# Sorted-block attention feeding a maxout MoE: the MoE of one batch interleaved with the attention of the next, v sorted from a rearranged copy, xT read strided from PSUM, q transposed in column tiles

## The chip, the cores and the metric

The kernel runs on one core of one Trainium2 chip. The time is the device time of one launch in microseconds (us). The engines of the core are TensorE (PE for its matmuls, PEld for its weight loads), VectorE (DVE), ScalarE (ACT), GpSimd (POOL) and SyncE (SP). A weight load puts the stationary operand into the array, and the matmul behind it streams the moving operand past it.

## The reference

With 4 batches, 8 heads, 768 positions and 64 dimensions per head, the positions are cut into 8 blocks of 96. A Sinkhorn iteration makes an 8 by 8 matrix P per head, P mixes the blocks of k and of v, each q block attends to the mixed k and v block of its own index, and the result feeds a two-way maxout layer. P is `sort_net` at the start.

```python
for _ in range(5):
    P = np.exp(P - P.max(-1, keepdims=True))
    P = P / (P.sum(-1, keepdims=True) + 1e-09)
    P = P / (P.sum(-2, keepdims=True) + 1e-09)
k_sorted = np.einsum('bhij,bhjcd->bhicd', P, k_b)     # v_sorted likewise
scores = scale * np.matmul(q_b, k_sb.transpose(0, 1, 2, 4, 3))
attn = softmax(scores)
x = np.matmul(attn, v_sb)                             # to (3072 tokens, 512)
g = np.maximum(x @ w1, x @ w2)                        # 512 -> 1024
out = g @ w_out                                       # 1024 -> 512
```

## The kernel before

The work is done per batch of 768 tokens; k and v are loaded and sorted for two batches at a time (`sb` 0 is batches 0 and 1, `sb` 1 is batches 2 and 3). max(h1, h2) is computed as h2 + relu(x(w1 - w2)), and h2 @ w_out is folded into one matrix wc = w2 @ w_out, so that the MoE has one hidden product (`moe_h`) and an output product with two parts (`moe_out`).

The order of all instructions is the order in which the Python code issues them (the schedule is manual). Each engine runs its own queue strictly in that order. All PSUM tiles share one pool of 4 buffers of two banks, used in rotation, so the fifth tile waits until the first has been copied out. The copies out of PSUM that go through `evac` (L81) are given to ACT or DVE by a running sum of estimated costs (`load`, `pick`, L72 to L79).

The parts are:

- The five Sinkhorn iterations (L167) and the building of the block-diagonal matrices `bd_v` and `bd_k` from P (L189 to L224), for both `sb` together, before anything else on PE.
- `q_transposes(b, half)` (L232): `pair_q` (L98) first lets DVE bring the two heads of a pair side by side, then 12 transposes of 128x128 per half put q into `qT`.
- `sort_k(sb, t)` (L254), 6 steps of 32 small matmuls in two diagonal quarters of the array, and `sort_v(sb, t)` (L275), 8 steps of 8 matmuls. The weights of a `sort_v` matmul are 96 columns of `v_raw`, 64 elements (128 bytes) apart: `vv[:, :, t * 8 + n]`.
- `scores(b, u)` (L294), 8 matmuls with weights of 64 rows and 96 columns, then one exponential on ACT. `values(b, u)` (L318), 8 matmuls with weights of 96 columns, then a reciprocal and a multiplication on DVE, which leave the tile `x`. A 65th column of ones in `v_sb` gives the softmax sum. There are 8 of each per batch.
- `x_transposes(b, hp)` (L347), 4 per batch: 8 transposes of `x` and one ACT copy into `xT` that brings the positions into order on the way. It reads PSUM in sequence and writes 2-byte elements 12 bytes apart.
- `w2_transposes`, `w_product` and `w_difference` (L371 to L411) make wc and w1 - w2 once.
- `moe_h(b, ch, t)` (L416), 8 per batch, and `moe_out(b, ti)` (L441), 6 per batch: 14 units per batch.

The top level (L490 to L554) does the attention of batches 0 and 1 with the weight work in between, then issues the 56 MoE units and hands out the list `rest` (sort of `sb` 1, attention of batches 2 and 3) between units 6 to 27, that is, within the MoE of batches 0 and 1. The MoE of batches 2 and 3 follow alone. In `attention_steps` (L478) `values` comes two steps behind its `scores`, and `x_transposes` directly behind the second of its two `values`.

All input loads are issued on POOL's queue in the order q of batch 0, k, v, q of batch 1, w2, w_out, w1; the loads for batches 2 and 3 follow as soon as their buffers are read out. The output is stored from SP's queue.

Of the kernel before, what the change touches and what calls it, by code (L numbers as in the profile page):

```python
# [15 lines left out]
def kernel(  # L16
# [80 lines left out]

    def pair_q(b):  # L98

        t = qpool.tile([128, HP, R, 2, D], BF16, tag="q_pair", name="q_pair")  # L100
        for par in range(2):
            nc.vector.tensor_copy(
                out=t[:, :, :, par, :],
                in_=q_raw[b].rearrange("p (a t) (r d) -> p a r t d", t=2, d=D)[:, :, :, par, :],
            )
# [76 lines left out]


    maskJ = const.tile([128, NB], FP32, tag="maskJ", name="maskJ")
    nc.vector.reduce_sum(
        out=maskJ, in_=ident.rearrange("p (m j) -> p j m", j=NB), axis=AX.X
    )
    bd_v, bd_k = [], []
    for sb in range(NSB):  # L189
        sel = const.tile([G, 2, 8, NB], BF16, tag=f"sel{sb}", name=f"sel{sb}")  # L190
        src = ident[0:G, sb * 16 : sb * 16 + 16].rearrange("p (gp par) -> p par gp", par=2)
        for par in range(2):
            nc.vector.tensor_copy(
                out=sel[:, par], in_=src[:, par, :].to_broadcast([G, 8, NB])
            )
# [151 lines left out]
    def x_transposes(b, hp):  # L347
        ps = ps_bf16("tx_ps")
        for ih in range(2):
# [235 lines left out]
```

## Time and profile before

| | us |
|---|---|
| median of three runs | 245.03 (244.81 to 247.16) |
| the profiled execution, whole | 243.13 |
| its span, from the first to the last instruction | 241.1 |
| PE busy in the span | 194.1 |
| ACT busy, DVE busy | 110.3, 88.2 |

[...] The whole time is 2.03 us longer than the span. The durations below come from that one execution.

### The profile page before, as it was taken

The page shows a single profiled execution, that of the slowest core. Times are in us where ns is not written, and L with a number is a line of the kernel's source. Part 1 is how long each engine was busy: PE and PEld are TensorE (multiplying, and loading weights), DVE is VectorE, ACT ScalarE, POOL GpSimd, SP SyncE. Part 2 cuts the span into 40 slices and gives each one's busy share as a digit, 9 for nine tenths or more (in the row PEclk, how much of TensorE's full clock was granted, in tenths as well). Part 3 has the DMA queues.
Part 4 walks back from the last instruction along what each step waited for, and adds up shares of the span by engine and source line. Part 5 has one row for each costly group of instructions (what it writes and reads, how often), then busy time and mean ns, then how long its engine had stood idle before and what let it go on. Part 6 is the DMA issues. An engine that isn't in the chain of part 4 may idle for free.

```text
span 241.1 us, 4147 instructions
## 1 busy us (share of the span) xinstructions
PE 194.1 (81%) x1846; PEld 128.2 (53%) x1858; DVE 88.2 (37%) x159; ACT 110.3 (46%) x98; POOL 18.1 (8%) x35
## 2 busy tenths in 40 slices
PE   0037697867869579999999677898979999999983
PEld 0036696756744435777765455654444654465431
DVE  4755275442620660523322545454133312023210
ACT  3108413977584275643152656946575320142010
POOL 8450312110000000000000000000000000000000
PEclk9999655575758959999999979999999999999999
DMA  5999999999800000000110200000120202220132
GB/s 70 211 222 200 210 205 209 211 223 203 138 3 0 0 0 3 3 4 13 74 58 32 87 3 0 0 3 23 67 87 6 84 0 87 87 90 0 48 126 87
DMA packets 11952, 19.13 MB, mean 79 GB/s; under 512 B 1696, under 2 KB 6816, under 8 KB 11680
## 3 DMA queue, kind: packets, MB, share of 16 engines
q0 software_dynamic: 8608, 12.59, 29.0%
q1 hardware_dynamic: 3328, 6.30, 6.8%
q8 instruction: 14, 0.23, 0.4%
q14 instruction: 2, 0.02, 0.0%
HBM read 25.17 MB, written 6.29 MB: 131 GB/s over the span
## 4 chain that ended last, share of the span: by engine, by line
PE 67%; DVE 15%; ACT 12%; issue 4%; DMA 1%; DVEq 0%; ACTq 0%
PE out_ps L458 17%; PE h_ps L422 16%; PE v_ps L279 9%; PE out_ps L450 8%; ACT xT L361 7%; DVE x L338 5%; PE o_ps L325 3%; PE wc_ps L395 3%; PE s_ps L301 3%; PE tx_ps L353 2%; PE tq_ps L239 2%; PE k_ps L262 2%; ACT kT L83 2%; PE tw_ps L375 1%; DVE o L85 1%
## 5 line engine op out<-in xcount | busy, mean ns | idle before, releaser
L361 ACT COPY xT<-tx_ps 128x768 bf16<-128x768 bf16 x16 | 43.5, 2722 | 25.2 <-PE tx_ps L353 25.2
L422 PE MATMUL h_ps<-xT,w_sb 128*128 128x384 bf16 x256 | 47.1, 341 | 1.0 <-DVE w_sb L405 0.9
L458 PE MATMUL out_ps<-wo_sb,g 128*128 128x512 bf16 x192 | 45.4, 379 | 0.1
L422 PEld LDWEIGHTS <-w_sb 128*128 128x128 bf16 x256 | 25.2, 101 | 19.1 <-issue 2.5
L309 ACT ACTIVATE e<-s_ps 96x768 bf16<-96x768 f32 x32 | 26.0, 845 | 12.2 <-PE s_ps L301 12.2
L458 PEld LDWEIGHTS <-g 128*128 128x128 bf16 x192 | 18.8, 98 | 22.7
L432 ACT ACTIVATE g<-h_ps 128x768 bf16<-128x768 f32 x21 | 17.4, 830 | 24.9 <-PE h_ps L422 24.9
L450 PE MATMUL out_ps<-wc,xT 128*128 128x512 bf16 x85 | 23.3, 379 | 1.4 <-DVE o L85 0.8
L353 PE MATMUL tx_ps<-ident,x 96*128 96x96 bf16 x128 | 12.2, 232 | 13.7 <-DVE x L338 12.8
L85 DVE COPY o<-out_ps 128x1024 f32<-128x1024 f32 (+1 forms) x8 | 9.3, 1158 | 36.2 <-PE out_ps L458 36.2
L338 DVE TENSOR_TENSOR x<-o_ps,rs 96x512 bf16<-96x512 f32 x32 | 22.0, 687 | 1.1
L325 PE MATMUL o_ps<-v_sb,e 96*96 96x65 bf16 x256 | 18.9, 225 | 4.1 <-ACT xT L361 2.5
L279 PEld LDWEIGHTS <-v_raw 128*96 128x96 bf16 x128 | 21.6, 257 | 0.5
L279 PE MATMUL v_ps<-bv,v_raw 128*96 128x128 bf16 x128 | 21.7, 347 | 0.0
L325 PEld LDWEIGHTS <-e 96*96 96x96 bf16 x256 | 16.9, 141 | 6.6 <-issue 2.5
L85 DVE CAST v_sb<-v_ps 96x1024 bf16<-96x1024 f32 x10 | 12.2, 1221 | 21.9 <-PE v_ps L279 21.6
L301 PE MATMUL s_ps<-qT,kT 64*96 64x96 bf16 x256 | 13.5, 240 | 6.9 <-issue 1.9
L434 DVE TENSOR_SCALAR g<-h_ps 128x768 bf16<-128x768 f32 x11 | 10.5, 958 | 21.0 <-PE h_ps L422 21.0
L83 ACT COPY o<-out_ps 128x1024 f32<-128x1024 f32 (+1 forms) x5 | 4.6, 927 | 28.0 <-PE out_ps L458 28.0
L336 DVE RECIPROCAL rs<-o_ps 96x8 f32<-96x8 f32 x32 | 6.4, 200 | 29.2 <-PE o_ps L325 29.1
L353 PEld LDWEIGHTS <-x 96*128 96x128 bf16 x128 | 7.9, 110 | 17.0 <-DVE x L338 15.6
L301 PEld LDWEIGHTS <-kT 64*96 64x96 bf16 x256 | 10.0, 144 | 11.2 <-issue 8.0
(51 smaller groups left out, 128.6 us busy)
## 6 DMA issues: line engine op xcount, KB each, us to landing
out_dram<-o SPq DMA_DIRECT2D x11, 512.0 KB, 2.8
q_raw<-in_q_dram POOLq DMA_DIRECT2D x4, 768.0 KB, 16.8
k_raw<-in_k_dram POOLq DMA_DIRECT2D x12, 256.0 KB, 12.2
v_raw<-in_v_dram POOLq DMA_DIRECT2D x4, 768.0 KB, 16.0
w_sb<-in_moe_w_dram POOLq DMA_DIRECT2D x4, 512.0 KB, 19.4
wo_sb<-in_moe_w_out_dram POOLq DMA_DIRECT2D x2, 512.0 KB, 21.8
out_dram<-o SPq DMA_DIRECT2D x2, 256.0 KB, 2.0
p_sb<-in_sort_net_dram SPq DMA_DIRECT2D x1, 8.0 KB, 1.6
```

The lines of the kernel that those rows point to most:

```text
L85: nc.vector.tensor_copy(out=out_ap, in_=in_ap)
L279: nc.tensor.matmul(ps[0:BLK, n * 128 : (n + 1) * 128], vv[:, :, t * 8 + n], bd_v[sb], start=True, stop=True,)
L301: nc.tensor.matmul(ps[0:BLK, h2 * 512 + ii * BLK : h2 * 512 + (ii + 1) * BLK], kT[h2 * 64 : h2 * 64 + 64, gp * 8 + i, :], qT[b][h2 * 64 : ...
L309: nc.scalar.activation(out=e, in_=ps[0:BLK].rearrange("p (t f) -> p t f", t=2)[:, :, 0 : 4 * BLK], func=AF.Exp, scale=scale,)
L325: nc.tensor.matmul(ps[0:BLK, h2 * 512 + ii * 65 : h2 * 512 + (ii + 1) * 65], e[:, h2, ii * BLK : (ii + 1) * BLK], v_sb[:, h2 * 64 + gp * 8 ...
L338: nc.vector.tensor_tensor(out=x.rearrange("p i t d -> p t i d"), in0=ov[:, :, :, 0:D], in1=rs.to_broadcast([BLK, 2, 4, D]), op=ALU.mult,)
L353: nc.tensor.matmul(ps[:, i * BLK : (i + 1) * BLK], x[:, ii].rearrange("p t d -> p (t d)"), ident[0:BLK, 0:BLK], is_transpose=True, start=True,
L361: nc.scalar.copy(out=xT[:, hp, b * S : (b + 1) * S].rearrange("p (i c r) -> p i r c", r=R, c=PB), in_=ps[:, 0:S].rearrange("p (i r c) -> p ...
L422: nc.tensor.matmul(ps[:, m * 512 : m * 512 + TCH], w1_sb[:, hp, fb * 128 : (fb + 1) * 128], xT[:, hp, tok0 : tok0 + TCH], start=(hp == 0), ...
L432: nc.scalar.activation(out=g, in_=src, func=AF.Relu)
L450: nc.tensor.matmul(dst, xT[:, hp, tok0 : tok0 + 128], wc[:, hp, :], start=(hp == 0), stop=False,)
L458: nc.tensor.matmul(dst, g_tiles[b, ch, fb // 2][:, fb % 2, off : off + 128], wo_sb[:, fb, :], start=False, stop=(fb == NFB - 1),)
```

## The change

- Order: only batch 0 is attended before the MoE begins. The attention of batch b+1 (for batch 2 with the sort of `sb` 1 ahead of it) is handed out between the 14 MoE units of batch b; the MoE of batch 3 stands alone.
- In `attention_steps`, `values` comes three steps behind its `scores`, and `x_transposes` at least one `values` behind its second `x`.
- v is first copied by `turn_v` into `v_dc`, where the 96 positions of one dimension lie together: 4 copies on DVE for `sb` 0, and 4 copies on POOL for `sb` 1, issued behind the load of the last q.
- The weights of `sort_v`, `scores` and `values` are read 128 columns wide (32 of them beyond the block, their results unused), so 32 spare columns are set to zero at the ends of `kT`, `v_dc` and of eight fixed `e` buffers that replace the pool.
- `q_transposes` no longer pairs heads on DVE; each 128x128 transpose becomes two with 64 columns of weights, which write the two halves of the PSUM partitions.
- `x_transposes` copies out with a strided read of PSUM and a write in sequence, by ACT or DVE as `evac` chooses.
- Sinkhorn and selections are interleaved, `bd_v` and `bd_k` are built separately for each `sb`, and q of batch 0 is transposed ahead of them. The identity and the mask are made ahead of the load of k.

```diff
-    def pair_q(b):
...
+    kT = big.tile([128, 64 * BLK + 32], BF16, tag="kT", name="kT")
+    nc.vector.memset(kT[:, 64 * BLK :], 0.0)
+    v_dc = big.tile([128, D * BLK + 32], BF16, tag="v_dc", name="v_dc")
...
         for n in range(2 * R):
             hp, r = half * 2 + n // R, n % R
-            nc.tensor.matmul(
-                ps[:, n * 128 : (n + 1) * 128],
-                q_pair[b][:, hp, r].rearrange("p t d -> p (t d)"),
+            for h2 in range(2):
+                nc.tensor.matmul(
+                    ps[h2 * 64 : h2 * 64 + 64, n * 128 : (n + 1) * 128],
+                    qv[:, 2 * hp + h2, r, :],
...
+    def turn_v(eng, t, parts):
+        n = D // parts
+        eng.tensor_copy(
+            out=v_dc[:, t * n * BLK : (t + 1) * n * BLK].rearrange("p (d c) -> p d c", c=BLK),
+            in_=v_raw.rearrange("p (c d) -> p d c", d=D)[:, t * n : (t + 1) * n, :],
+        )
...
-                ps[0:BLK, n * 128 : (n + 1) * 128],
-                vv[:, :, t * 8 + n],
+                ps[:, n * 128 : (n + 1) * 128],
+                v_dc[:, (t * 8 + n) * BLK : (t * 8 + n) * BLK + 128],
                 bd_v[sb],
...
-                    kT[h2 * 64 : h2 * 64 + 64, gp * 8 + i, :],
+                    kT[h2 * 64 : h2 * 64 + 64, (gp * 8 + i) * BLK : (gp * 8 + i) * BLK + 128],
...
-                    e[:, h2, ii * BLK : (ii + 1) * BLK],
+                    e[:, (h2 * 4 + ii) * BLK : (h2 * 4 + ii) * BLK + 128],
...
-        nc.scalar.copy(
-            out=xT[:, hp, b * S : (b + 1) * S].rearrange("p (i c r) -> p i r c", r=R, c=PB),
-            in_=ps[:, 0:S].rearrange("p (i r c) -> p i r c", r=R, c=PB),
-        )
-        load["A"] += 800
+        evac(
+            xT[:, hp, b * S : (b + 1) * S].rearrange("p (i c r) -> p i c r", r=R, c=PB),
+            ps[:, 0:S].rearrange("p (i r c) -> p i c r", r=R, c=PB),
+            S,
+        )
...
-        for u in range(8 + 2):
+        for u in range(8 + 4):
             if u < 8:
                 steps.append(lambda u=u: scores(b, u))
-            if u >= 2:
-                steps.append(lambda u=u: values(b, u - 2))
-                if u % 2 == 1:
-                    steps.append(lambda u=u: x_transposes(b, (u - 2) // 2))
+            if 3 <= u < 8 + 3:
+                steps.append(lambda u=u: values(b, u - 3))
+            if u >= 5 and u % 2 == 1:
+                steps.append(lambda u=u: x_transposes(b, (u - 5) // 2))
...
+    for t in range(4):
+        turn_v(nc.vector, t, 4)
     for t in range(8):
         sort_v(0, t)
+        if t % 2 == 1:
+            scores(0, 4 + t // 2)
+    for u in range(8):
         values(0, u)
+        if u >= 2 and u % 2 == 0:
+            x_transposes(0, u // 2 - 1)
     for t in range(2):
         w2_transposes(t)
+    x_transposes(0, 3)
     for t in range(2):
         w_product(t)
     load_q(2)
     load_k(1, 3)
     load_v(1)
     load_q(3)
+    for t in range(4):
+        turn_v(nc.gpsimd, t, 4)
     for t in range(2):
         w_difference(t)
+    between = [
+        q_steps(1) + attention_steps(1),
+        q_steps(2) + sort_steps(1) + attention_steps(2),
+        q_steps(3) + attention_steps(3),
+        [],
+    ]
     for b in range(B):
...
+        steps, done = between[b], 0
+        for n, unit in enumerate(units):
+            unit()
+            want = -(-len(steps) * (n + 1) // (len(units) - 1))
+            while done < min(want, len(steps)):
+                steps[done]()
+                done += 1
```

DVE's queue around the first sort of v, ahead of the first `values`: kT, v_sb and v_dc are copies, rs and x belong to `values`. Before:

```order
L85 COPY qT<-tq_ps 128x1536
L85 CAST kT<-k_ps 128x64x16 x2
L85 CAST v_sb<-v_ps 96x128x8 x6
L336 RECIPROCAL rs<-o_ps 96x8
L338 TENSOR_TENSOR x<-o_ps,rs 96x2x4x64
```

And now:

```order
L85 CAST kT<-k_ps 128x64x16 x3
L202 TENSOR_TENSOR pm_452<-pe,maskJ 128x64
L209 TENSOR_REDUCE pt_454<-pm_452 128x8
L211 TENSOR_TENSOR bv_456<-mask_92,pt_454 128x128
L218 TENSOR_TENSOR bk_458<-bv_456 128x64
L285 COPY v_dc<-v_raw 128x1536 x4
L85 CAST v_sb<-v_ps 96x128x8 x6
L350 RECIPROCAL rs<-o_ps 96x8
L352 TENSOR_TENSOR x<-o_ps,rs 96x2x4x64
```

All four turning copies stand ahead of all six of DVE's casts of sorted v, in the same queue.

POOL's queue at its end: the loads, w_sb being w1 and w2. Before:

```order
L138 DMA w_sb<-in_moe_w_dram 128x2x1024 x2
L95 DMA q_raw<-in_q_dram 128x8x384
L118 DMA k_raw<-in_k_dram 64x1x2048 x6
L125 DMA v_raw<-in_v_dram 64x1x6144 x2
L95 DMA q_raw<-in_q_dram 128x8x384
```

And now:

```order
L127 DMA w_sb<-in_moe_w_dram 128x2x1024 x2
L95 DMA q_raw<-in_q_dram 128x8x384
L107 DMA k_raw<-in_k_dram 64x1x2048 x6
L114 DMA v_raw<-in_v_dram 64x1x6144 x2
L95 DMA q_raw<-in_q_dram 128x8x384
L285 COPY v_dc<-v_raw 128x1536 x4
```

The four copies of the second v stand behind the load of the last q, whose buffer is read by the q transposes of batch 1.

PE's queue where the transposes of an attention begin that runs beside the MoE, with buffer numbers. Before, in batch 2: the second x that tx_ps_1723 takes is made from o_ps_1710.

```order
L325 MATMUL o_ps_1710<-v_sb_182,e_1613 96x65
L325 LDWEIGHTS e_1613
L325 MATMUL o_ps_1710<-v_sb_182,e_1613 96x65
L353 LDWEIGHTS x_1686
L353 MATMUL tx_ps_1723<-ident_96,x_1686 128x96
```

And now, in batch 1: the second x that tx_ps_1087 takes, x_1040, is made from o_ps_1029.

```order
L436 MATMUL h_ps_1076<-xT_138,w1_sb_82 128x384
L436 LDWEIGHTS w1_sb_82
L436 MATMUL h_ps_1076<-xT_138,w1_sb_82 128x384
L367 LDWEIGHTS x_1006
L367 MATMUL tx_ps_1087<-ident_87,x_1006 128x96
```

Before, the transposes followed at once on the product that the second x comes from; now h_ps_1042, s_ps_1053, o_ps_1063 and h_ps_1076 stand between o_ps_1029 and them.

## Rows read from the trace of the kernel before

**Rows 1.** Busy time by engine in stretches: us, PE, PEld, DVE, ACT, POOL, clock, DMA.

```profile
39.00:59.00 20.00, 14.72 (x181) 12.86 (x182) 9.21 (x20) 15.33 (x12) 2.82 (x5) 0.59 1.14 215
...
71.00:87.00 16.00, 12.14 (x85) 6.19 (x84) 6.60 (x11) 7.92 (x4) 0.00 (x0) 0.82 0.00 0
...
124.00:184.40 60.40, 50.89 (x507) 31.32 (x511) 23.96 (x43) 38.34 (x30) 0.00 (x0) 0.97 0.09 36
184.40:237.40 53.00, 51.97 (x269) 26.47 (x271) 11.34 (x11) 10.44 (x14) 0.00 (x0) 1.00 0.17 65
237.40:241.10 3.70, 0.00 (x0) 0.00 (x0) 0.00 (x0) 0.58 (x1) 0.00 (x0) 0.97 0.18 71
```

**Rows 2.** Who waited for whom: us in total, times, longest.

```profile
PE tx_ps L353 <- DVE x L338: 12.8, 17, 1.6
```

**Rows 3.** Groups by line and shape: busy us, mean ns | idle before, releaser.

```profile
L361 ACT COPY xT<-tx_ps 128x768 bf16<-128x768 bf16 x16 | 43.5, 2722 | 25.2 <-PE tx_ps L353 25.2
L338 DVE TENSOR_TENSOR x<-o_ps,rs 96x512 bf16<-96x512 f32 x32 | 22.0, 687 | 1.1
L336 DVE RECIPROCAL rs<-o_ps 96x8 f32<-96x8 f32 x32 | 6.4, 200 | 29.2 <-PE o_ps L325 29.1
L434 DVE TENSOR_SCALAR g<-h_ps 128x768 bf16<-128x768 f32 x11 | 10.5, 958 | 21.0 <-PE h_ps L422 21.0
L85 DVE CAST v_sb<-v_ps 96x1024 bf16<-96x1024 f32 x10 | 12.2, 1221 | 21.9 <-PE v_ps L279 21.6
L83 ACT CAST v_sb<-v_ps 96x1024 bf16<-96x1024 f32 x6 | 6.1, 1021 | 16.7 <-PE v_ps L279 16.7
L102 DVE COPY q_pair<-q_raw 128x1536 bf16<-128x1536 bf16 x8 | 4.3, 573 | 0.2 <-issue 0.2
L279 PEld LDWEIGHTS <-v_raw 128*96 128x96 bf16 x128 | 21.6, 257 | 0.5
L325 PEld LDWEIGHTS <-e 96*96 96x96 bf16 x256 | 16.9, 141 | 6.6 <-issue 2.5 <-DVE v_sb L85 1.5 <-ACT e L309 0.2
L422 PEld LDWEIGHTS <-w_sb 128*128 128x128 bf16 x256 | 25.2, 101 | 19.1 <-issue 2.5 <-DVE w_sb L405 1.8
```

**Rows 4.** POOL in order of time: start, us, what [idle before, releaser].

```profile
5.63 0.29 POOL masks.py:197 MEMSET ident<- 128x128 bf16 x1
...
24.02 0.71 POOL L138 DMA_DIRECT2D w_sb<-in_moe_w_dram  x1 [6.58 <-DMA v_raw<-in_v_dram]
```

**Rows 5.** The chain that ended last, in order of time: start, us, what.

```profile
59.48 3.43 PE tw_ps L375 x32
...
71.97 7.48 PE wc_ps L395 x30
79.48 1.23 DVE wc L85
...
84.84 2.36 DVE w_sb L405 x2
...
96.58 1.34 PE tq_ps L239 x24
...
99.22 1.64 PE k_ps L262 x96
...
184.53 10.40 PE h_ps L422 x64
...
210.47 10.40 PE h_ps L422 x64
```

**Rows 6.** PE in order of time, 171.2 to 172.8 us: start, us, what.

```profile
171.21 0.38 PE L301 MATMUL s_ps<-qT,kT 64*96 64x96 bf16 x8
171.52 0.55 PE L325 MATMUL o_ps<-v_sb,e 96*96 96x65 bf16 x8
171.90 1.03 PE L450 MATMUL out_ps<-wc,xT 128*128 128x512 bf16 x4
```

**Rows 7.** Input loads by line: count, KB each, median us from issue to landing.

```profile
w_sb<-in_moe_w_dram POOLq DMA_DIRECT2D x4, 512.0 KB, 19.4
```

More of the change, by code (lines that the diff above doesn't have):

```diff
@@ L89 @@
     nc.sync.dma_start(out=p_sb, in_=sort_net.rearrange("b h i j -> (b h) i j"))
-    q_raw, q_pair, qT = {}, {}, {}
+    q_raw, qT = {}, {}
     def load_q(b):
@@ L96, in load_q @@
         q_raw[b] = t
-    def pair_q(b):
[L100 to L104, printed above, removed]
-            )
-        load["D"] += 1000
-        q_pair[b] = t
     k_raw = big.tile([128, BLK * D], BF16, tag="k_raw", name="k_raw")
@@ L166, with sinkhorn @@
     p_bf = const.tile([G, NB, NB], BF16, tag="p_bf", name="p_bf")
-    for it in range(5):
+    maskJ = const.tile([128, NB], FP32, tag="maskJ", name="maskJ")
+    sels = []
+    def sinkhorn(it):
         nc.scalar.activation(out=p_sb, in_=p_sb, func=AF.Exp)
@@ L181, with selections, block_diagonals @@
         )
[L184 to L195, printed above, removed]
+    def selections():
+        nc.vector.reduce_sum(
+            out=maskJ, in_=ident.rearrange("p (m j) -> p j m", j=NB), axis=AX.X
+        )
+        for sb in range(NSB):
+            sel = const.tile([G, 2, 8, NB], BF16, tag=f"sel{sb}", name=f"sel{sb}")
+            src = ident[0:G, sb * 16 : sb * 16 + 16].rearrange("p (gp par) -> p par gp", par=2)
+            for par in range(2):
+                nc.vector.tensor_copy(
+                    out=sel[:, par], in_=src[:, par, :].to_broadcast([G, 8, NB])
+                )
+            sels.append(sel)
+    bd_v, bd_k = {}, {}
+    def block_diagonals(sb):
         pe = ps_f32("pe")
@@ L307, in scores @@
                 )
-        e = epool.tile([BLK, 2, 4 * BLK], BF16, tag="e", name="e")
+        e = e_bufs[(b * 8 + u) % NE]
         nc.scalar.activation(
-            out=e,
+            out=e[:, 0 : 8 * BLK].rearrange("p (t f) -> p t f", t=2),
             in_=ps[0:BLK].rearrange("p (t f) -> p t f", t=2)[:, :, 0 : 4 * BLK],
@@ L526 @@
     load_q(3)
+    for t in range(4):
+        turn_v(nc.gpsimd, t, 4)
     for t in range(2):
         w_difference(t)
-    rest = []
-    for half in range(2):
-        rest.append(lambda half=half: q_transposes(2, half))
-    for t in range(6):
-        rest.append(lambda t=t: sort_k(1, t))
-    for t in range(8):
-        rest.append(lambda t=t: sort_v(1, t))
-    rest += attention_steps(2)
-    for half in range(2):
-        rest.append(lambda half=half: q_transposes(3, half))
-    rest += attention_steps(3)
-    units = []
-    for b in range(B):
-        units += [lambda b=b, t=t: moe_h(b, 0, t) for t in range(4)]
-        units += [lambda b=b, t=t: moe_h(b, 1, t) for t in range(4)]
-        units += [lambda b=b, ti=ti: moe_out(b, ti, b == B - 1 and ti >= 4) for ti in range(6)]
-    hold, span = 5, 2 * 14 - 1
-    done = 0
-    for n, unit in enumerate(units):
-        unit()
-        want = len(rest) * max(0, n + 1 - hold) // (span - hold)
-        while done < min(want, len(rest)):
-            rest[done]()
-            done += 1
+    between = [
[3 more added lines that the diff above has]
+        [],
+    ]
+    for b in range(B):
+        units = [lambda t=t: moe_h(b, 0, t) for t in range(4)]
+        units += [lambda t=t: moe_h(b, 1, t) for t in range(4)]
+        units += [lambda ti=ti: moe_out(b, ti, b == B - 1 and ti >= 4) for ti in range(6)]
+        steps, done = between[b], 0
[5 more added lines that the diff above has]
+                done += 1
 _INS = ['q', 'k', 'v', 'sort_net', 'moe_w1', 'moe_w2', 'moe_w_out']
```

68 lines of the change are left out of this document (32 added, 36 removed).

## The prediction

> **What bounds the kernel now.** I read the table of busy time by stretch first, then the waits, then the groups by line. In the last 53 us, the MoE of batches 2 and 3, PE is busy 51.97 us at the full clock [rows 1]: PE is the bound there and nothing beside it matters. [...] The waits name whom: x transposes waited for DVE's `x` 17 times, 12.8 us in all [rows 2], since they follow directly on the product that `x` is made from. The groups by line name the second: the ACT copy into xT takes 2722 ns for 768 elements, where the DVE pass over 768 elements of g takes 958 [rows 3]. So the MoE units are solid, and the time to be had lies in the attention and in all that comes before the first MoE unit, which starts behind the two `w_difference` passes, at 84.84 + 2.36 = 87.2 us [rows 5].
>
> **The change, along the time of the new order.** The new time is built up stage by stage, since nearly everything moves.
>
> *Until v is there.* POOL's load queue shows the first v load landed at 24.0 us, by the wait that ended then [rows 4]. The order of loads up to there is the same, and the identity and mask that go ahead of k cost POOL about 1 us while the load of q is still running, so I keep 24.0. Sinkhorn, q transposes, the sort of k and the first four scores move about among themselves before that, and I give them no gain: v is late next.
>
> *Turning v on DVE.* Four copies of 1536 elements, which no row shows with this read 128 bytes apart. From the g pass (768 elements, 958 ns) and the v_sb cast (1024, 1221 ns) an element costs 1.03 ns, so that 1536 take 958 + 768 x 1.03 = 1.75 us [rows 3]. Below, the q_pair copy of 1536 elements in runs of 64 took 0.57 us [rows 3]. Above, the weight load of v with the same spacing took 257 ns against 141 ns for as many columns in sequence, a factor of 1.8, which gives 3.2 us [rows 3]. I take 1.75, the nearest kind: 4 x 1.75 = 7.0 us, to 31.0. The bounds are 2.3 and 12.8 us.
> [...]
>
> *Sorted v, batch 0.* The casts of v_sb: DVE has six of them behind its four copies, 6 x 1.22 = 7.3 us [rows 3], and 0.4 for the last to get its matmuls: 38.7. On PE the 64 matmuls go from a pace set by the 257 ns strided loads to one of contiguous 128-column loads, which take 101 ns in the MoE [rows 3], but PE is not what is waited for. So the first sort of v hardly ends earlier than it did; what the faster matmuls win here the turning takes.
>
> *Attention of batch 0, wc, w1 - w2.* Eight times 0.69 + 0.20 on DVE = 7.1 us [rows 3], and 1.2 for the first product and the transposes that break the run: 47.0. w2 transposes 3.43 [rows 5]; their copies are now both on ACT, 2048 elements, twice the 1.02 of its 1024-element cast [rows 3], the second one after the first: 3.4 + 0.3 + 2.0, to 52.7. The last x transposes fit beside it. w_product: 30 of its 32 matmuls took 7.48 [rows 5], so 8.0, to 60.7. Its second half is cast by DVE, and both `w_difference` passes are queued behind that cast, with PE's first MoE unit behind them: 1.23 + 2.36 [rows 5] + 0.3 for the hand-overs, to 64.6. Weights are no hindrance: the last w1 load, issued at 24.02, lands some 19.4 us later, at 43.4 [rows 4, 7]. The MoE begins at 64.6 in place of 87.2, with one attention more to do behind it.
>
> *MoE.* A batch takes 210.47 - 184.53 = 25.94 us [rows 5]; four: 103.8. Unchanged.
>
> *Three attentions between MoE units.* On PE at the full clock scores took 171.52 - 171.21 = 0.31 and values 171.90 - 171.52 = 0.38 us [rows 6]. Both now load 128 columns, which took 101 ns where 96 took 141 [rows 3]. Of scores (96 columns streamed by two halves of the rows) at most half goes, of values 31/96, as 65 columns are streamed against 96 loaded; if a wider load costs by its width, both grow by a third. So 0.16 to 0.41 and 0.26 to 0.51; I take 0.28 and 0.31. An x transposition step streams 8 x 96 columns as scores do, 0.31. The q transposes took 1.34 us for 24 [rows 5]; 48 with half the weights take between 1.34, if the two halves of the columns run side by side, and 2.7; I take 2.0. Per attention 8 x 0.28 + 8 x 0.31 + 4 x 0.31 + 2.0 = 8.0, three times 24.0; bounds 17.8 and 33.9 us.
>
> *Sort of batches 2 and 3.* k as it was: 192 matmuls at 1.64 per 96, 3.3 us; v: 64 matmuls of 128 columns at the q transposes' 1.34/24, 3.6 us [rows 5]. Together 6.9. Before, this v sort ran at the pace of its 257 ns loads.
>
> *Waits that stay.* 60.4 - 50.89 = 9.5 us of idle PE for two attentions [rows 1] is 4.75 each, of which 12.8/4 = 3.2 was the wait for `x` [rows 2]. That wait goes, as a `values` and a MoE unit now lie between, and the 2.7 us copies that held PSUM buffers and ACT go too (16 x 1.8 us off ACT and DVE together). What is left is 1.55 each, 4.7 for three. I add 2 for the head of each interleaved batch, where g, the two q copies and four exponentials stand in a row on ACT and DVE, and for the lower clock behind the wait for `w_difference`. The pair copies on DVE, 8 x 0.57 [rows 3], were beside PE and are worth nothing more. The two single MoE batches took 53.0 against 2 x 25.94, so 1.1 for the last outputs, and 3.7 from the last matmul to the end [rows 1].
>
> *Sum.* 64.6 + 103.8 + 24.0 + 6.9 + 4.7 + 2 + 1.1 + 3.7 = 210.8 us of span, against 241.1. The whole is 243.13 - 241.1 = 2.03 longer: 212.8. The median of the runs shown, 245.03, is 1.9 above the profiled execution, so **214.7, I say 215 us**.
>
> **Rivals.**
>
> *Wide loads and half-array transposes cost by their width.* For it: nothing in the trace has 64-column transposes on all 128 rows or loads of 128 columns on 64 rows. Against it: the 101 ns row. Then the three attentions take 33.9 and not 24.0: 215 + 9.9 = 225.
>
> *The interleaved attention still stalls.* For it: four PSUM buffers serve everything, and ACT alone has all exponentials. If each attention keeps its 4.75 us, and not 1.55: 215 + 9.6 = 225. Against it: the wait that made most of it is named in the rows and is moved out of the way.
>
> *POOL is too slow with the second v: slower than before.* Its four copies stand behind the load of the last q, which waits for the q transposes of batch 1, at about 64.6 + 1.3 + 2.0 = 68, and 69 when it is issued. PE's queue reaches the second sort of v at about 64.6 + 25.9 + 8 + 2 for the first MoE with its attention, and 3.9 + 2.0 + 3.3 for what stands ahead of it in the second: 110. So POOL has 41 us, 10 us per copy, before PE waits for it, and everything behind stands in the same queue. The one price of POOL in the rows is the fill of 128 columns in 0.29 us [rows 4], 2.3 ns per element, 3.5 us for 1536, or 6.3 with the factor 1.8 of a strided read. The time would be level with before at 41 + 30 = 71 us, 18 us per copy, and at 22 us per copy 215 + 88 - 41 = 262.
> [...]
>
> *The change does not do what it says.* The part that could fall flat is the sort of batch 0, and the sum already gives it nothing.
>
> **How the numbers follow.** Forecast 0.72, its own range 204 to 223 (turning at its lower bound -4.7, attentions at theirs -6.2, or +5.8 with the turning at its upper). The wide loads 0.12, the stalls 0.12, POOL 0.04. The range for 8 in 10 takes in the first two rivals: 203 to 229. Faster by over 1% 0.95, within 1% 0.01 and slower by over 1% 0.04; 1% is about what a measurement of this kernel can tell, as its three runs lie 0.9% apart.
>
> **What would show it.** First MoE matmul near 65 us; turning copies near 1.75 us; xT copies under 1 us; waits of x transposes for `x` under 3 us in all from there on; a v sort of some 56 ns per matmul in the second MoE; the last two MoE-only marks, 25.9 us for batch 3. The prediction is wrong if the first MoE matmul comes after 72 us, if PE idles more than 12 us between there and the last batch, or if PE stands still in front of the second sort of v.

## The result and the profile after

The changed kernel takes 205.86 us, median of 4 runs (204.32 to 206.02), against 244.92 for the kernel before, run beside it: a ratio of 0.8408, interval 0.8346 to 0.847. The profiled execution took 205.96 us, with a span of 204.1. That is inside the forecast range and 9.1 us below the forecast of 215.

The busy time of the engines, from the head of the page; PE is now busy for 84% of the span:

```profile
PE 170.8 (84%) x1942; PEld 106.2 (52%) x1954; DVE 92.1 (45%) x170; ACT 78.8 (39%) x93; POOL 30.6 (15%) x39
```

The busy time by stretch, with the columns of [rows 1]. The clock is the one granted to TensorE, as a share of its full one; in the traces of before and after it stands at 0.50 (after, 60.5 to 63.5 us) or at 1.00 (after, 50.05 to 56.27), and a value between is the mean over a stretch. The first two rows are the turning and sorting of v and what follows it up to the MoE; then come the three stretches with a MoE and an attention in one another.

```profile
24.30:37.40 13.10, 8.48 (x96) 7.27 (x97) 12.65 (x10) 6.05 (x9) 4.51 (x6) 0.87 1.21 210
37.40:59.80 22.40, 16.56 (x161) 11.01 (x161) 11.22 (x20) 7.78 (x8) 2.17 (x4) 0.85 1.13 214
59.80:94.80 35.00, 34.72 (x339) 19.96 (x343) 12.60 (x22) 15.48 (x18) 12.08 (x5) 0.95 0.26 57
94.80:139.60 44.80, 41.28 (x598) 26.28 (x600) 22.80 (x31) 21.03 (x24) 0.00 (x0) 1.00 0.10 37
139.60:173.30 33.70, 33.49 (x342) 19.09 (x344) 13.46 (x23) 14.42 (x18) 0.00 (x0) 1.00 0.13 48
```

From the first MoE unit on PE is now the bound nearly everywhere: idle 0.28, 3.52 and 0.21 us in the three mixed stretches, 4.0 together, where two attentions before cost 9.5 [rows 1]. In the first 59.8 us it still isn't.

The waits of PE that are left of [rows 2] (who waits, for whom: us, times, longest):

```profile
PE tx_ps L367 <- DVE x L352: 3.7, 6, 1.5
```

The groups that answer to [rows 3], with its columns:

```profile
L83 ACT COPY xT<-tx_ps 128x768 bf16<-128x768 bf16 x11 | 8.8, 799 | 18.2 <-PE tx_ps L367 18.2
L285 DVE COPY v_dc<-v_raw 128x1536 bf16<-128x1536 bf16 x4 | 5.9, 1525 | 1.1 <-DMA v_raw<-in_v_dram 1.1
L285 POOL COPY v_dc<-v_raw 128x1536 bf16<-128x1536 bf16 x4 | 11.2, 2838 | 0.0
L339 PEld LDWEIGHTS <-e 96*128 96x128 bf16 x256 | 11.3, 103 | 3.3 <-DVE v_sb L85 0.5 <-issue 0.3
L293 PEld LDWEIGHTS <-v_dc 128*128 128x128 bf16 x128 | 9.9, 117 | 3.9 <-DVE v_dc L285 2.1 <-issue 0.8
```

Reading PSUM strided and writing xT in sequence costs ACT 799 ns where writing it strided cost 2722; `e` is loaded in 103 ns at 128 columns where 96 took 141; the load of turned v takes 117 ns where the strided one took 257.

PE and DVE in order of time in the first 64 us and PE further on (start, us, what, idle before and releaser; each fence is one engine):

```profile
24.34 5.86 DVE L285 COPY v_dc<-v_raw 128x1536 bf16<-128x1536 bf16 x4 [1.08 <-DMA v_raw<-in_v_dram]
30.14 6.86 DVE L85 CAST v_sb<-v_ps 96x1024 bf16<-96x1024 f32 x6
...
44.89 0.69 DVE L352 TENSOR_TENSOR x<-o_ps,rs 96x512 bf16<-96x512 f32 x1
...
56.30 1.23 DVE L85 CAST wc<-wc_ps 128x1024 bf16<-128x1024 f32 x1 [7.60 <-PE wc_ps L409]
57.44 2.35 DVE L419 TENSOR_TENSOR w_sb<-w_sb 128x2048 bf16<-128x2048 bf16 x2
```

```profile
37.48 1.12 PE L339 MATMUL o_ps<-v_sb,e 96*128 96x65 bf16 x24 [0.83 <-ACT v_sb L83]
...
44.43 2.94 PE L389 MATMUL tw_ps<-ident,w_sb 128*128 128x128 bf16 x32
...
48.28 1.04 PE L409 MATMUL wc_ps<-wo_sb,w2T 128*128 128x512 bf16 x3 [0.57 <-ACT w2T L83]
50.05 6.22 PE L409 MATMUL wc_ps<-wo_sb,w2T 128*128 128x512 bf16 x28 [0.73 <-ACT w2T L83]
58.71 0.50 PE L436 MATMUL h_ps<-xT,w_sb 128*128 128x384 bf16 x2 [2.45 <-DVE w_sb L419]
59.85 1.84 PE L436 MATMUL h_ps<-xT,w_sb 128*128 128x384 bf16 x6 [0.64 <-DVE w_sb L419]
61.62 2.44 PE L246 MATMUL tq_ps<-ident,q_raw 128*64 128x128 bf16 x48
...
79.54 0.34 PE L315 MATMUL s_ps<-qT,kT 64*128 64x96 bf16 x8
79.81 0.43 PE L339 MATMUL o_ps<-v_sb,e 96*128 96x65 bf16 x8
80.08 1.03 PE L464 MATMUL out_ps<-wc,xT 128*128 128x512 bf16 x4
...
96.22 1.53 PE L246 MATMUL tq_ps<-ident,q_raw 128*64 128x128 bf16 x48
97.68 0.69 PE L269 MATMUL k_ps<-bk,k_raw 64*64 64x64 bf16 x32
...
105.64 1.50 PE L293 MATMUL v_ps<-bv,v_dc 128*128 128x128 bf16 x24
...
198.46 1.89 PE L472 MATMUL out_ps<-wo_sb,g 128*128 128x512 bf16 x8
```

In front of the MoE PE waits 2.45 and 0.64 us for `w_difference`. The MoE begins at 58.71 and is under way at 59.85, where before it began at 87.2 [rows 5]. Differences of starts give 0.27 us for scores and 0.27 for values (0.31 and 0.38 before [rows 6]), and 1.46 for a batch's 48 q transposes. Batch 3 takes from 173.31 to 198.46 + 1.89 = 200.35, 27.0 us, as forecast (25.94 and 1.1 for the last outputs). Of the waits for `x` two fall between MoE units, the longer of them 1.52 us at 132.64.

### The profile page after: what moved, and what is told of

The parts are those of the page before. It is cut to its first block, busy times and chain, and to the rows that moved or that the text cites. A ratio compares the mean times of both kernels' runs of the same rounds, so it can differ in the third digit from the quotient of the medians.

```text
span 204.1 us, 4340 instructions
## 1 busy us (share of the span) xinstructions
PE 170.8 (84%) x1942; PEld 106.2 (52%) x1954; DVE 92.1 (45%) x170; ACT 78.8 (39%) x93; POOL 30.6 (15%) x39
## 4 chain that ended last, share of the span: by engine, by line
PE 69%; DMA 11%; DVE 10%; ACT 6%; issue 2%; DVEq 0%; POOLq 0%; ACTq 0%
PE out_ps L472 21%; PE h_ps L436 19%; PE out_ps L464 10%; DMA v_raw<-in_v_dram 8%; PE o_ps L339 4%; DMA q_raw<-in_q_dram 4%; PE v_ps L293 3%; PE wc_ps L409 3%; DVE v_dc L285 3%; PE tx_ps L367 3%; PE tq_ps L246 2%; DVE x L352 2%; PE s_ps L315 2%; ACT w2T L83 2%; PE k_ps L269 2%
## 5 line engine op out<-in xcount | busy, mean ns | idle before, releaser
L83 ACT COPY xT<-tx_ps 128x768 bf16<-128x768 bf16 x11 | 8.8, 799 | 18.2 <-PE tx_ps L367 18.2
L246 PE MATMUL tq_ps<-ident,q_raw 128*64 128x128 bf16 x192 | 8.3, 261 | 8.7 <-DMA q_raw<-in_q_dram 8.7
L339 PE MATMUL o_ps<-v_sb,e 96*128 96x65 bf16 x256 | 13.5, 202 | 0.9 <-ACT v_sb L83 0.8
L293 PE MATMUL v_ps<-bv,v_dc 128*128 128x128 bf16 x128 | 11.4, 257 | 2.7 <-DVE v_dc L285 1.9
L339 PEld LDWEIGHTS <-e 96*128 96x128 bf16 x256 | 11.3, 103 | 3.3 <-DVE v_sb L85 0.5
L464 PEld LDWEIGHTS <-xT 128*128 128x128 bf16 x96 | 8.3, 97 | 8.7 <-issue 1.7
L246 PEld LDWEIGHTS <-q_raw 128*64 128x64 bf16 x192 | 7.5, 138 | 9.9 <-DMA q_raw<-in_q_dram 8.7
L315 PE MATMUL s_ps<-qT,kT 64*128 64x96 bf16 x256 | 10.4, 218 | 2.8 <-DVE v_sb L85 1.5
L269 PE MATMUL k_ps<-bk,k_raw 64*64 64x64 bf16 x384 | 9.1, 215 | 3.7 <-issue 2.0
L293 PEld LDWEIGHTS <-v_dc 128*128 128x128 bf16 x128 | 9.9, 117 | 3.9 <-DVE v_dc L285 2.1
```

The lines of the kernel that those rows point to most:

```text
L83: nc.scalar.copy(out=out_ap, in_=in_ap)
L246: nc.tensor.matmul(ps[h2 * 64 : h2 * 64 + 64, n * 128 : (n + 1) * 128], qv[:, 2 * hp + h2, r, :], ident, is_transpose=True, start=True, st ...
L293: nc.tensor.matmul(ps[:, n * 128 : (n + 1) * 128], v_dc[:, (t * 8 + n) * BLK : (t * 8 + n) * BLK + 128], bd_v[sb], start=True, stop=True,)
L315: nc.tensor.matmul(ps[:, h2 * 512 + ii * BLK : h2 * 512 + (ii + 1) * BLK], kT[h2 * 64 : h2 * 64 + 64, (gp * 8 + i) * BLK : (gp * 8 + i) * ...
L339: nc.tensor.matmul(ps[:, h2 * 512 + ii * 65 : h2 * 512 + (ii + 1) * 65], e[:, (h2 * 4 + ii) * BLK : (h2 * 4 + ii) * BLK + 128], v_sb[:, h2 ...
L464: nc.tensor.matmul(dst, xT[:, hp, tok0 : tok0 + 128], wc[:, hp, :], start=(hp == 0), stop=False,)
```

## The experiments

"After" is the changed kernel. Every ratio is to the kernel before, run on the same chip; after stands at 0.8408 (0.8346 to 0.847). Six kernels each undo one part.

**e1: xT written strided by ACT again.**

```diff
-        evac(
-            xT[:, hp, b * S : (b + 1) * S].rearrange("p (i c r) -> p i c r", r=R, c=PB),
-            ps[:, 0:S].rearrange("p (i r c) -> p i c r", r=R, c=PB),
+        nc.scalar.copy(
+            out=xT[:, hp, b * S : (b + 1) * S].rearrange("p (i c r) -> p i r c", r=R, c=PB),
+            in_=ps[:, 0:S].rearrange("p (i r c) -> p i r c", r=R, c=PB),
...
+        load["A"] += 800
```

> Undoes one part of the change: xT is again copied by ACT with a write 12 bytes apart, 2.72 us a copy in place of 0.80. Theory A (the time came from the order and from PE's own pace, a slow copy beside PE is hidden): within 4 us of the changed kernel's 205.9, since 12 of the 16 copies lie beside MoE units of 1.3 to 2.6 us and values follow their scores by some 5 us. Rival B (ACT and the PSUM buffers that a slow copy holds were what stalled PE): 12 copies x 1.9 us, at least half of it on PE's path, 217 us or more.

Measured: 207.32 us, 0.8492 (0.8429 to 0.8555). The interval overlaps that of after, so the sum alone doesn't tell it from no loss. It lies where theory A had it, but the reason that theory A gave, a copy hidden beside PE, doesn't hold. The edit also shifts the sharing-out between ACT and DVE: DVE casts the first half of wc, `w_difference` then runs beside the second half of w_product, and the MoE starts at 57.34 in place of 59.85. When 8 MoE matmuls and 48 transposes are done, at 60.20 in e1 and at 63.99 in after, e1 still takes 206.0 - 60.20 = 145.8 us to the end of the span, after 204.1 - 63.99 = 140.1. Of the 5.7 us lost there, 4.3 are seen as waits of PE for the copies, of which after has 0.2:

```profile
PE out_ps L464 <- ACT xT L375: 4.3, 3, 2.2
```

That the whole is only 1.5 us longer is luck: the earlier start, which the edit wasn't made for, pays most of it back.

**e2: v not turned, sorted from the strided columns as before.**

```diff
-                v_dc[:, (t * 8 + n) * BLK : (t * 8 + n) * BLK + 128],
+                v_raw.rearrange("p (c d) -> p c d", d=D)[:, :, t * 8 + n],
...
-    for t in range(4):
-        turn_v(nc.vector, t, 4)
...
-    for t in range(4):
-        turn_v(nc.gpsimd, t, 4)
```

> Undoes the rearranged copy of v: no turn_v, sort_v loads 96 columns 128 bytes apart from v_raw, as the kernel before. Theory A (in the first sort the turning takes what the faster matmuls win; only the second sort, beside the MoE, wins): MoE begins within 2 us of the 59.8 of the changed kernel, the second sort's 64 matmuls take 0.17 us each and not 0.056, 7.3 us more, so 211 to 215 us. Rival B (turning pays in both places): MoE begins 4 us later or more and the whole is 217 or more. Rival C (the second sort is held by its 8 copies out of PSUM, not by PE): the whole within 3 us of 205.9.

Measured: 213.69 us, 0.8757 (0.8703 to 0.8812). PE in order of time, behind the first sort and in the second:

```profile
38.06 1.48 PE L339 MATMUL o_ps<-v_sb,e 96*128 96x65 bf16 x24 [0.67 <-ACT v_sb L83]
...
107.18 4.02 PE L293 MATMUL v_ps<-bv,v_raw 128*96 128x128 bf16 x24
```

In batch 0 the first product starts at 38.06 against 37.48: the turning costs DVE 5.9 us there and brings that product only 0.6 us forward. The gain is in the second sort, where POOL turns v beside PE: 4.02 against 1.50 us for 24 matmuls, 64/24 x 2.52 = 6.7 us.

**e3: 96-column weights in scores, values and the sort of v.**

```diff
-                    e[:, (h2 * 4 + ii) * BLK : (h2 * 4 + ii) * BLK + 128],
+                    e[:, (h2 * 4 + ii) * BLK : (h2 * 4 + ii + 1) * BLK],
```

(and the same in the other two).

> Undoes the 128-column weights of scores, values and sort_v: 96 columns, everything else as changed. Theory A (a 96-column load sets the pace of these matmuls, a 128-column load does not): values go back from 0.27 to some 0.36 to 0.38 us per step and scores from 0.28 to 0.31, that is 24 x 0.13 = 3 us beside the MoE, and up to 1 us before it, so 208 to 210 us. Rival B (the pace comes from elsewhere): step times as changed and a whole within 1 us of 205.9.

Measured: 209.16 us, 0.8553 (0.8502 to 0.8604). PE in order of time:

```profile
121.27 0.38 PE L315 MATMUL s_ps<-qT,kT 64*96 64x96 bf16 x8
121.58 0.55 PE L339 MATMUL o_ps<-v_sb,e 96*96 96x65 bf16 x8
121.96 1.03 PE L464 MATMUL out_ps<-wc,xT 128*128 128x512 bf16 x4
```

```profile
L339 PEld LDWEIGHTS <-e 96*96 96x96 bf16 x256 | 15.6, 135 | 2.6 <-DVE v_sb L85 0.5 <-issue 0.3
```

Scores are back at 0.31 us and values at 0.38, as before [rows 6]: 8 x (0.04 + 0.11) = 1.2 us per attention, 3.6 for the three between MoE units, against 3.3 measured. The first rival, a price by width, is refuted for the loads: the wider load is the shorter one, 103 ns for 128 columns of `e` where the group of 96 in e3, the last line above, has 135.

**e4: products two steps behind their scores, transposes straight behind their product.**

```diff
-        for u in range(8 + 4):
+        for u in range(8 + 2):
...
-            if 3 <= u < 8 + 3:
-                steps.append(lambda u=u: values(b, u - 3))
-            if u >= 5 and u % 2 == 1:
-                steps.append(lambda u=u: x_transposes(b, (u - 5) // 2))
+            if u >= 2:
+                steps.append(lambda u=u: values(b, u - 2))
+                if u % 2 == 1:
+                    steps.append(lambda u=u: x_transposes(b, (u - 2) // 2))
```

> Undoes the distances in the attention that runs beside the MoE: values two steps behind their scores, x transposes directly behind the second of their values. Theory A (that wait was 3.2 us per attention and comes back): 12 transposes wait about 0.8 to 1.6 us each for x, 10 to 13 us more, 215 to 219 us. Rival B (the wait comes back, but a thinner interleave with MoE units absorbs most): 3 to 6 us more, 209 to 212. Rival C (it no longer matters): within 2 us of 205.9.

Measured: 217.24 us, 0.8885 (0.8819 to 0.895). The wait of [rows 2] is back:

```profile
PE tx_ps L367 <- DVE x L352: 14.0, 14, 1.8
```

14.0 - 3.7 = 10.3 of the 11.4 us are this one wait. MoE units between the steps alone don't hide it; the distance does.

**e5: the order of before at the top level, with all the new parts.** With this order the x transposes of batches 0 and 1 also stand straight behind their product again.

```diff
...
+    for u in range(4, 8):
+        scores(1, u - 4)
         values(0, u)
...
+    for u in range(4, 8):
+        scores(1, u)
+        values(1, u - 4)
...
+    rest += attention_steps(2)
...
+    rest += attention_steps(3)
```

> Undoes the order alone: the top level of the kernel before (attention of batches 0 and 1 ahead of the MoE, the sort and attention of batches 2 and 3 within the MoE of batches 0 and 1), with every other part as changed, the wider distances in the interleaved attentions too. Theory A (moving one attention beside the MoE is worth the time that it took alone at half clock less the 7 us that it costs PE beside the MoE): the first MoE matmul comes at 72 to 76 us in place of 59, and the whole is 10 us or more above the 205.9 of the changed kernel, 216 us or more. Rival B (with cheap xT copies and close loads the attention of batch 1 would be nearly as cheap alone): 206 to 210 us. The two meet between.

Measured: 219.27 us, 0.8972 (0.8933 to 0.9011). The attention of batches 0 and 1 ahead of the MoE runs at a granted clock of 0.67, with PE idle for 4.5 of 24 us. The stretch (columns of [rows 1]), then PE at the head of the MoE, then PE's waits for `x`:

```profile
37.00:61.00 24.00, 19.48 (x301) 15.52 (x298) 15.06 (x28) 13.62 (x16) 3.10 (x5) 0.67 1.12 212
```

```profile
78.16 9.88 PE L436 MATMUL h_ps<-xT,w_sb 128*128 128x384 bf16 x46 [0.31 <-DVE w_sb L419]
```

```profile
PE tx_ps L367 <- DVE x L352: 9.3, 13, 1.6
```

The MoE starts 18.3 us later than in after (78.16 against 59.85). Of that one attention of 7 to 8 us is not to be done later; the rest, 10 to 11, is most of the 13.4 lost. The order isn't alone in that. Of the 9.3 us of waits for `x`, 6.3 lie ahead of the MoE, where after has 1.3: some 5 us go with the close steps, which e4 prices beside the MoE.

**e6: POOL's four copies made six times over.**

```diff
-    for t in range(4):
-        turn_v(nc.gpsimd, t, 4)
+    for rep in range(6):
+        for t in range(4):
+            turn_v(nc.gpsimd, t, 4)
```

> Makes POOL do its four copies of the second v six times over, some 67 us in place of 11.2. Theory A (POOL's copies have cover until PE reaches the second sort of v at 103.9 us, and beyond that cost one for one): they end near 65.3 + 67 = 132 us, the first quarter's last copy near 124, so the second sort of v starts 18 to 22 us later and the whole is 222 to 228 us. Rival B (POOL's copies also slow VectorE or the rest while they run): MoE units between 65 and 103 us run slower than the 1.3 and 2.6 us that they take, and the whole is more than 228. Rival C (other work stands between and absorbs the wait): under 218.

Measured: 227.29 us, one run. POOL is here as slow as the third rival asks. POOL, then PE, in order of time:

```profile
64.45 66.12 POOL L285 COPY v_dc<-v_raw 128x1536 bf16<-128x1536 bf16 x24
```

```profile
122.30 1.04 PE L293 MATMUL v_ps<-bv,v_dc 128*128 128x128 bf16 x8 [18.89 <-POOL v_dc L285]
123.13 2.77 PE L436 MATMUL h_ps<-xT,w_sb 128*128 128x384 bf16 x8
```

PE stands 18.9 us in front of the second sort, as that rival had it; the MoE unit behind the stand takes 2.77 us, where such a unit took 1.46 in e8 (below). In after the four copies take 11.2 us in all; the last begins at 73.6 (its row stands under e12) and ends some 27 us ahead of its use at 103.88. The MoE units that ran beside the 66 us, up to the stand, were no slower: 8 matmuls of h in 1.46 to 1.48 us, in after 1.46 to 1.48.

**e7: pair copies and full-width q transposes back.**

```diff
         if half == 0:
+            pair_q(b)
...
-            for h2 in range(2):
-                nc.tensor.matmul(
-                    ps[h2 * 64 : h2 * 64 + 64, n * 128 : (n + 1) * 128],
-                    qv[:, 2 * hp + h2, r, :],
+            nc.tensor.matmul(
+                ps[:, n * 128 : (n + 1) * 128],
+                q_pair[b][:, hp, r].rearrange("p t d -> p (t d)"),
```

> Undoes the q transposes: pairs are formed by two DVE copies and 24 transposes of 128 columns follow, in place of 48 of 64 columns. Theory A (48 narrow transposes go in nearly the time of 24 wide ones, 1.46 against 1.33 us, and the pairing lies beside other work): within 1.5 us of 205.9, either side; q transposes take 1.33 us where the clock is full. Rival B (the pairing is waited for at the head of each interleaved batch, as the pair copies stand behind the casts of the MoE on DVE): 1 us or more per batch, 208.5 to 211 us.

Measured: 209.37 us, 0.8581 (0.8548 to 0.8615): 3.5 us lost, and my theory A fell. PE's wait in the profile, PE in order of time, and DVE at the second place:

```profile
PE tq_ps L255 <- DVE q_pair L102: 14.5, 2, 12.4
```

```profile
12.45 2.74 PE L255 MATMUL tq_ps<-ident,q_pair 128*128 128x128 bf16 x24 [12.45 <-DVE q_pair L102]
...
99.98 1.24 PE L255 MATMUL tq_ps<-ident,q_pair 128*128 128x128 bf16 x19 [2.06 <-DVE q_pair L102]
```

```profile
98.03 0.96 DVE L457 TENSOR_SCALAR g<-h_ps 128x768 bf16<-128x768 f32 x1 [5.97 <-PE h_ps L445]
98.90 1.02 DVE L102 COPY q_pair<-q_raw 128x1536 bf16<-128x1536 bf16 x2
```

At the start the pair copies stand on DVE behind the five Sinkhorn iterations (they begin at 11.38), and the transposes begin at 12.45, where after begins at 8.69, on the landing of q; the MoE is under way 1.6 us later (61.48). In the second MoE the copy stands on DVE behind a g pass that waits for PE, and PE waits 2.06 us for the copy. At the heads of batches 1 and 3 it doesn't wait, so rival B's number holds and its 1 us per batch doesn't. 48 transposes of half the width take 1.46 us in after, 24 of the full one 1.34 [rows 5], so PE's own work isn't the difference.

Five kernels follow what the profile of after left open.

**e8: `w_difference` ahead of `w_product`.** It needs only the weights, and its wait is 3.1 us of PE.

```diff
     for t in range(2):
+        w_difference(t)
+    for t in range(2):
         w_product(t)
...
-    for t in range(2):
-        w_difference(t)
```

> Moves the two w_difference passes ahead of w_product in the code, so that DVE does them while PE makes wc. Theory A (in the changed kernel PE stood 3.1 us at the head of the MoE, waiting for nothing else): the first MoE matmul follows on w_product at about 56.5 us in place of 58.7 and 59.85, and the whole is 2.5 to 3.5 us less, 202.4 to 203.4 us. Rival B (the two q copies and the exponentials behind it on ACT then take the place of that wait): less than 1.5 us gained, 204.5 or more.

Measured: 201.36 us, 0.8242 (0.8212 to 0.8272): 4.5 us, more than expected. PE in order of time, then a stretch of e8 and one of after with much the same work, 8 (in after 6) MoE matmuls and 48 transposes:

```profile
56.01 1.46 PE L436 MATMUL h_ps<-xT,w_sb 128*128 128x384 bf16 x8
```

```profile
56.00:58.87 2.87, 2.87 (x58) 2.06 (x56) 0.57 (x1) 1.82 (x2) 0.00 (x0) 1.00 1.01 214
```

```profile
59.85:63.99 4.14, 4.14 (x54) 2.94 (x55) 0.00 (x0) 1.65 (x2) 0.00 (x0) 0.59 0.11 21
```

The MoE starts 3.84 us earlier, and at the ends of these stretches, 58.87 and 63.99, where both have done 8 MoE matmuls and 48 transposes, the lead is 5.1. The rest is the clock: behind its wait after runs at 0.59, most of it at 0.50, and takes 4.14 us; e8, which doesn't stop, runs at 1.00 and takes 2.87.

The wait alone doesn't decide the clock. PE makes the same stop of 2.45 and 0.64 us for `w_difference` in seven traces. In after, e2, e3, e4, e7 and e12 the stretch behind it runs at 0.59 to 0.63 (the first 6 MoE matmuls take 1.84 us in after, 1.61 in e2, 1.91 in e4 and 2.10 in e7), but in e6 at 1.00 (1.15 us):

```profile
60.63:63.17 2.54, 2.54 (x54) 1.87 (x55) 0.00 (x0) 1.36 (x2) 0.00 (x0) 1.00 0.05 10
```

The same 6 MoE matmuls and 48 transposes take 2.54 us there and 4.14 in after, so the lower clock costs 1.6 us. The traces without the stop (e1, e8, e9, e11) have 1.00. Why e6 kept the full clock no run shows.

**e9: e8, and the turning copies among the casts they hold up.**

```diff
-    for t in range(4):
-        turn_v(nc.vector, t, 4)
     for t in range(8):
+        for n in {0: (0, 1), 2: (2,), 4: (3,)}.get(t, ()):
+            turn_v(nc.vector, n, 4)
+            load["D"] += 1450
         sort_v(0, t)
```

> With the early w_difference, the turning copies of the first v stand among the casts in DVE's queue (two ahead, the third behind the second sort step, the fourth behind the fourth), and the costs that share out the copies count 1450 ns for each, so that ACT and DVE take four casts of v_sb each. Theory A (the stretch from v's landing to the first values is DVE's queue, 5.9 + 6 x 1.15 us): the first values come 1.5 to 2.5 us earlier than the 37.4 of the early w_difference, the whole 199 to 200 us against 201.4. Rival B (PSUM buffers, held until the casts, are the limit): no gain, 201 or more.

Measured: 199.74 us, 0.8162 (0.8125 to 0.8199), 1.6 below e8. The first product starts at 36.45, 1.0 earlier than in after, less than expected; it waits for the last cast, on DVE.

Each turn can't go just ahead of its own sort step, since the last matmul of a quarter reads 32 columns of the next; so the first two stand together.

**e10: e8, and the w2 transposes among the products of batch 0.**

```diff
-    for t in range(2):
-        w2_transposes(t)
+        if u in (2, 4):
+            w2_transposes(u // 2 - 1)
```

> With the early w_difference, the two w2_transposes stand among the values of batch 0 in place of behind them. Theory A (values of batch 0 are paced by DVE, 8 x 0.84 us, and PE and ACT have room beside it): w_product begins some 3 us earlier and the whole is 198 to 199 us against 201.4. Rival B (their four uses of ACT and of PSUM buffers hold up the values): less than 1 us gained, 200.5 or more.

Measured: 202.42 us (200.78 to 204.42), 0.825 (0.8198 to 0.8301): no gain over e8 that could be told, so the expectation fell. Its only trace is that of the longest run, 204.42, and doesn't speak for the others. e11, which is e9 with this edit, starts its MoE 1.1 us earlier than e9 in the traces, but their medians aren't told apart; what the edit is worth in the whole stays open.

**e11: e8, e9 and e10 together.** The edit is the three above.

> The two edits before and the early w_difference together. Theory A (they lie one behind the other on the way to the first MoE unit, so their gains add): 196 to 198 us. Rival B (the landing of the weights or of the next loads takes the place of what is removed): 199 or more.

Measured: 199.04 us (198.35 to 200.98, 6 runs), 0.8151 (0.8107 to 0.8196). It isn't told apart from e9, whose interval it overlaps, and misses what theory A expected. Rival B has the number but not the reason: PE waits for no load behind that of the first q. In its profile the MoE starts at 53.87, 2.1 us ahead of e8, and w_product, with 7.07 us for 31 matmuls, keeps the full clock.

By their intervals e8, e9 and e11 are faster than both kernels.

**e12: the turning copies read v in sequence.** The copies stay, the rearrangement is left out.

```diff
-            in_=v_raw.rearrange("p (c d) -> p d c", d=D)[:, t * n : (t + 1) * n, :],
+            in_=v_raw.rearrange("p (d c) -> p d c", c=BLK)[:, t * n : (t + 1) * n, :],
```

> The changed kernel with turning copies that read v in sequence; the rearrangement of v is left out. It measures the read 128 bytes apart by itself. Theory A (the strided read costs, the rest is a plain copy): DVE's copies fall from 1.46 to about 0.55 us, as the pair copies of 1536 elements had, POOL's from 2.83 to 2 us or less, and the first MoE matmul comes up to 3 us earlier. Rival B (DVE copies at one element per cycle whatever the spacing): 1.4 us and more.

Measured: 202.12 us, one run. The copies by tile (shortest/median/longest ns, from when to when), of e12 and then of after:

```profile
L285 DVE COPY v_dc<-v_raw x4: 542/558/923, 24.4 to 26.2; 128x1536 bf16<-128x1536 bf16 x4
L285 POOL COPY v_dc<-v_raw x4: 1464/1469/1470, 61.8 to 66.0; 128x1536 bf16<-128x1536 bf16 x4
```

```profile
L285 DVE COPY v_dc<-v_raw x4: 1452/1456/1735, 24.3 to 28.8; 128x1536 bf16<-128x1536 bf16 x4
L285 POOL COPY v_dc<-v_raw x4: 2827/2831/2861, 65.3 to 73.6; 128x1536 bf16<-128x1536 bf16 x4
```

The spacing costs DVE 0.9 us per copy and POOL 1.4. DVE's is on the path: 3.5 us over the four, the MoE is under way 3.9 earlier (55.92), and the whole is 3.7 shorter. POOL's is hidden.

## Why the prediction was right, and where it was off

Right in direction and, but for one step, in mechanism; the forecast is too long by 9.1 us. By its own steps, each read between the starts of the rows above:

| step | predicted | measured |
|---|---|---|
| until v is there | 24.0 | 24.3 |
| turning v on DVE | 7.0 | 5.9 |
| casts, to the first product | 7.7 | 7.3 (30.2 to 37.48) |
| attention of batch 0 | 8.3 | 6.95 (to 44.43, where the next row begins) |
| w2 transposes and copies | 5.7 | 5.6 (to 50.05) |
| w_product | 8.0 | 6.2 (to 56.3) |
| wc cast and `w_difference` | 3.9 | 3.6 (to 59.85) |
| first MoE | 64.6 | 59.85 |
| from there to the last matmul | 142.5 | 140.5 (to 200.35) |
| to the span's end | 3.7 | 3.75 |

**The stage ahead of the MoE, 4.8 us.** Three terms make most of it. The turning copies took 1.46 us, the first 1.74, and not 1.75 each. In the attention of batch 0 the length was right, and what I had wrong was an overlap: DVE is done with the last `x` at 44.89 + 0.69 = 45.58, 8.1 us behind the first product, where I had 8.3. I let the w2 transposes begin behind that; they stand in PE's queue ahead of the last x transposes and begin 1.15 us before DVE is done. w_product was taken as starting whole behind the second w2T copy; three of its matmuls ran at 48.28, behind the first copy, and the other 28 took 6.22 at the full clock where the row I scaled had 7.48 for 30, at a granted clock of 0.89. That "the first sort of v hardly ends earlier" was right for the turning, whose part e2 puts at 0.6 us; the first product as a whole comes 1.9 us earlier than in before (37.48 against 39.34).

**From the MoE on, 2.0 us.** Per attention 8 x 0.27 + 8 x 0.27 + 4 x 0.34 + 1.46 = 7.1 us against 8.0, where an x transposition step took 0.34 (forecast 0.31); most of the difference is the q transposes, 1.46 and not 2.0, and values, 0.27 and not 0.31. The waits that stay, 4.7, came out at 4.0, under the 12 that would have refuted the forecast. The second v sort went at 1.50/24 = 62 ns with its hand-over, 56 without (1.34 for 24 in the chain), as forecast. The 2 us that I added for the heads and the lower clock: the clock alone took 1.6 (after against e6, under e8). With four times 25.94, the second sort at 7.1 and 1.1 at the end, these terms add up to 139.0; the last 1.5 of the 140.5 I have not placed.

**The median, 2 us.** I put the median of before above its profiled run by 1.9 and carried that over; after's median lies 0.1 below its profiled run. The whole is 1.86 longer than the span against 2.03. The upper end of the forecast's own range, 223, doesn't come out of the terms given for it: 214.7 + 5.8 is 220.5.

**One step was wrong.** "The pair copies on DVE, 8 x 0.57, were beside PE and are worth nothing more." In before PE did wait for them once, at its start:

```profile
PE tq_ps L239 <- DVE q_pair L102: 2.5, 1, 2.5
```

In the new order e7 loses 3.5 us to them, in two places: at the start, where they stand on DVE behind Sinkhorn, and at the head of batch 2, where they stand behind a g pass that waits for PE. I had priced the copies by their length and not by what stands ahead of them in DVE's queue.

**The rivals.** Price by width: refuted for the loads by e3 (103 ns for 128 columns, 135 for 96), and for the half-array transposes by 48 in 1.46 us, where 24 of the full width took 1.34 [rows 5]. The interleaved attention stalls: it would have, at the old distance of steps (e4: 10.3 us more of waits), and hardly does at the new one (two waits for `x`, 2.4 us in all). POOL too slow: its condition is real (e6), its price was 2.8 us per copy where the cover allows 10. The four took 11.2 us in the trace, and e12 has a factor of 1.9 for the spacing, 2.83 us against 1.47.

**What the parts are worth.** The six undoings lose, in medians, 1.5 (e1), 7.8 (e2), 3.3 (e3), 11.4 (e4), 13.4 (e5) and 3.5 (e7), 40.9 together, where the change gained 39.1. The two sums being close doesn't show that the parts don't overlap. e5 takes in some 5 us of close steps, e1's 1.5 isn't told from nothing, and the new order of Sinkhorn and of the building of `bd_v` and `bd_k` wasn't undone by itself. The order and the distance of the steps are the largest parts.

## What to carry to other kernels

When two stages are interleaved, count for each step how far behind its producer it stands: with MoE units between them but the old distance of the steps, PE waited 10.3 us more (e4). A copy on an engine with idle time is priced by when its turn comes in that engine's queue and by who waits for it, not by its length (e7). An operation without inputs from the stage ahead goes first if a long run waits for it: `w_difference` moved forward gave 4.5 us, most of it the 3.84 by which the MoE starts earlier (e8).

## What the runs showed of the hardware

- A copy of 1536 two-byte elements read 128 bytes apart from SBUF took DVE 1.46 us against 0.56 in sequence, and POOL 2.83 against 1.47 (e12). ACT's copy of 768 elements into xT took 2.72 us with the stride on the write [rows 3], and 0.80 with the stride on the read from PSUM.
- A weight load of 128 columns took 101 ns on 64 rows and 103 on 96 (after); with 96 columns the same two loads took 133 and 135 (e3).
- Two 64-column transposes into the two halves of the PSUM rows cost hardly more than one of 128: 48 in 1.46 us, 24 in 1.34 [rows 5].
- After PE had waited 2.45 and 0.64 us for `w_difference`, the granted clock was 0.59 to 0.63 in the next 3.8 to 4.1 us in six traces of seven, and 1.00 in the seventh (e6). Without the wait it was 1.00 (e1, e8, e9, e11). At 0.59 the same 54 matmuls took 4.14 us and not 2.54.
